# Per-row statistics and the tail copy as tensor_reduce, scores scaled at the PSUM copy, norm over 640 columns

## The chip, the cores and the metric

The kernel runs on one core of a Trainium2 chip. The metric is the device time in microseconds of one execution. The core has five engines that matter here: TensorE (PE, with its weight loads shown as PEld), VectorE (DVE), ScalarE (ACT), GpSimd (POOL) and the queue that issues DMAs (SP). Each runs its own instructions in order, and they meet at semaphores.

## The reference

Three stages follow each other. Attention has 4 batches of 8 heads, 576 rows and a head size of 64; it keeps only the 32 largest scores of each row:

```python
scores = scale * np.matmul(q, k.transpose(0, 1, 3, 2))      # scale = 1/8
kth = np.partition(scores, -top_k, axis=-1)[..., -top_k:-top_k + 1]
scores = np.where(scores >= kth, scores, -1000000000.0)
scores = scores - np.max(scores, axis=-1, keepdims=True)
attn = np.exp(scores)
attn = attn / (np.sum(attn, axis=-1, keepdims=True) + 1e-09)
out = np.matmul(attn, v)
```

Its output, 2304 tokens of 512 features, goes through a gated layer (`h = x @ w_in`, `h * sigmoid(h)`, `@ w_out`, inner width 2048), and then through `((x @ w1) * (x @ w2)) @ w3 @ w_out` with an inner width of 1024.

## The kernel before, in words

The 2304 tokens are cut into six blocks (`BLOCKS`) of three tiles of 128 rows. For each block the eight heads give 24 tiles of scores, taken two at a time: a **pair**, 72 of them in all. Blocks 0 and 1 are "native": their attention runs in plain float32. Blocks 2 to 5 split every operand into a rounded high part and a low rest, and multiply those.

The program writes its own order. `at(tick, order, fn)` puts a piece of work on a tick; a pair owns `SLOT = 7` ticks. After each tick the dense layers of the previous block (`mlp`, lines 645 to 647 for the first products of each layer, 766 for the last one) give a share of their steps, so that TensorE alternates between the two. During the first stretch these shares are the folding of `w3 @ w_out` (line 231) and the conversion of the weights (lines 134 to 202). After that, a scheduler in the compiler may still let an instruction pass another that would wait; each engine then runs the resulting list in order.

A pair goes through these steps:

- `plan_scores`: TensorE multiplies q and k (lines 412, 414, 415) into a PSUM bank, and `evac` (line 418) on ScalarE copies 288 columns into the score tile `st`.
- `plan_topk`, `mx` and `mr` (lines 445, 449) on VectorE: four rounds of MAX8 give the 32 largest values of a row in `top`, with three rounds of MATCH_REPLACE8 between them on the scratch tile `wk`.
- `bias` (lines 454, 455) on VectorE: `nt`, minus one eighth of the 32nd value, and `nb`, minus one eighth of the largest value less `nt`. Each handles 128 rows by 2 columns, a column for each tile of the pair.
- `mask` (line 463) and `ex` (line 469) on ScalarE: a Prelu with scale 1/8 and bias `nt` sends all that is below the 32nd value far down, and an Exp with bias `nb` follows, with the row's sum into `sm`.
- `recip` (lines 473, 474, 477) on VectorE: 1e-9 is added to `sm`, the reciprocal goes into `rc`; in the split blocks columns 512 to 575 of `e` times `rc` are written a second time, into columns 576 to 639.
- `norm` (lines 484, 486): columns 0 to 575 of `e` times `rc`, on ScalarE in the first four pairs and on GpSimd in the others.
- `plan_av`: two ticks or more later TensorE transposes `e` (lines 539 to 543), ScalarE copies it out (lines 549, 556, 557), GpSimd forms the low part (line 559), and TensorE multiplies with v (lines 572, 583).

GpSimd also forms the low parts of the dense layers' inputs (lines 660, 705), of q (line 335) and of k (line 340). All DMAs are issued by SP.

Of the kernel before, what the change touches and what calls it, by code (L numbers as in the profile page):

```python
# [8 lines left out]
FP32 = mybir.dt.float32  # L9
# [2 lines left out]
I32 = mybir.dt.int32  # L12
ACTF = mybir.ActivationFunctionType
ALU = mybir.AluOpType

TOPK = 32

# [12 lines left out]
SLOT = 7  # L30
NATIVE = lambda j: j < 2
# [19 lines left out]
def attention_moe_moe2_kernel(  # L51
# [13 lines left out]
    nc = tc.nc  # L65
    B, H, D2, S = qT.shape
# [7 lines left out]
    KC = (S + 127) // 128  # L74
    NFULL = S // 128
    HS = S // 2
    scale = 1.0 / float(D) ** 0.5
    NB = len(BLOCKS)

    w4_p = ctx.enter_context(tc.tile_pool(name="w4", bufs=1))  # L80
# [6 lines left out]
    s_p = ctx.enter_context(tc.tile_pool(name="s", bufs=2))  # L87
# [16 lines left out]
    def done(b):  # L104
        held.pop(id(b))
        free_banks.append(b)
# [4 lines left out]
    zero = w4_p.tile([128, 128], FP32R, name="zero")  # L111

    low = w4_p.tile([128, 1], FP32, name="low")
    n_conv = [0]


# [11 lines left out]
    def convert_scale(r, fold):  # L128
# [6 lines left out]
        else:  # L135
            nc.gpsimd.tensor_scalar(t, h, SHIFT, 1.0, op0=ALU.mult, op1=ALU.mult)

# [6 lines left out]
    def convert_bits(r, t_):  # L144
# [3 lines left out]
        nc.vector.scalar_tensor_tensor(out=wb, in0=tb, scalar=3, in1=r[:, :, 0],  # L148
                                       op0=ALU.logical_shift_left, op1=ALU.bitwise_or)
        if bits:  # L150
            nc.vector.scalar_tensor_tensor(out=wb, in0=r[:, :, 1], scalar=0x80000000, in1=wb,
                                           op0=ALU.bitwise_and, op1=ALU.bitwise_or)
        else:
            nc.gpsimd.tensor_tensor(out=w, in0=w, in1=r[:, :, 1].bitcast(FP32), op=ALU.mult)
        return w
# [122 lines left out]
    def at(tick, order, fn):  # L278
        plan.setdefault(tick, []).append((order, len(plan.get(tick, ())), fn))
# [110 lines left out]
    tiles = {}  # L390

    def plan_scores(n, base):
        items = []
        for j, h, i in pairs[n]:
            t0, T = blocks[j]
            for half in range(2):
                for si, (off, n_, b, s) in enumerate(runs(t0, T)):
                    a, e = max(off, i * 128), min(off + n_, (i + 1) * 128)
                    if a < e:
                        items.append((j, h, i, half, si, a - i * 128, e - i * 128))  # L400

        def go(tick, j, h, i, half, si, r0, r1):
            hd = heads[j, h]
            if n not in tiles:
                tiles[n] = s_p.tile([128, 2, S], FP32, tag="st", bufs=SB, name="st")
            m = pairs[n].index((j, h, i))
            kk = hd["k"][si][0]
            ps = bank("s")
            cs = slice(half * HS, (half + 1) * HS)
            q_ = hd["q"][:, i * 128:(i + 1) * 128]  # L410
            if NATIVE(j):
                nc.tensor.matmul(ps[:, 0:HS], lhsT=q_[0:D], rhs=kk[0:D, 0, cs], start=True, stop=True)  # L412
            else:
                nc.tensor.matmul(ps[:, 0:HS], lhsT=q_, rhs=kk[:, 0, cs], start=True, stop=False)  # L414
                nc.tensor.matmul(ps[:, 0:HS], lhsT=q_, rhs=kk[:, 1, cs], start=False, stop=True)  # L415

            def evac():
                nc.scalar.copy(out=tiles[n][r0:r1, m, cs], in_=ps[r0:r1, 0:HS])  # L418
                done(ps)

            at(tick + 1, 0, evac)

        for x, item in enumerate(items):
            tk = base + x * (SLOT - 1) // len(items)
            at(tk, 2, lambda tk=tk, item=item: go(tk, *item))

    def plan_topk(n, base):
        pr = pairs[n]
        m = len(pr)
        st = {}  # L430
        NR = TOPK // 8

        def begin():
            st["top"] = s_p.tile([128, 2, TOPK], FP32, tag="top", name="top")
            st["nt"] = s_p.tile([128, 2], FP32, tag="nt", name="nt")
            st["nb"] = s_p.tile([128, 2], FP32, tag="nb", name="nb")
            st["sm"] = s_p.tile([128, 2], FP32, tag="sm", name="sm")
            st["rc"] = s_p.tile([128, 2], FP32, tag="rc", name="rc")
            st["wk"] = s_p.tile([128, 2, S], FP32, tag="wk", bufs=1, name="wk")
            st["s"] = tiles[n]  # L440
            st["e"] = []

        def mx(r):
            for i in range(m):
                nc.vector.max(out=st["top"][:, i, r * 8:r * 8 + 8], in_=st["s" if r == 0 else "wk"][:, i])  # L445

        def mr(r):
            for i in range(m):
                nc.vector.match_replace(out=st["wk"][:, i], in_to_replace=st["top"][:, i, r * 8:r * 8 + 8],  # L449
                                        in_values=st["s" if r == 0 else "wk"][:, i], imm_value=-3.0e38)  # L450

        def bias():

            nc.vector.tensor_scalar(st["nt"][:, 0:m], st["top"][:, 0:m, TOPK - 1], -scale, 1.0, op0=ALU.mult, op1=ALU.mult)  # L454
            nc.vector.scalar_tensor_tensor(out=st["nb"][:, 0:m], in0=st["top"][:, 0:m, 0], scalar=-scale,  # L455
                                           in1=st["nt"][:, 0:m], op0=ALU.mult, op1=ALU.subtract)

        def mask():

            for i in range(m):  # L460
                e = s_p.tile([128, KC * 128], FP32, tag="e", bufs=EB, name="e")
                st["e"].append(e)
                nc.scalar.activation(out=e[:, 0:S], in_=st["s"][:, i], func=ACTF.Prelu, scale=scale,  # L463
                                     bias=st["nt"][:, i:i + 1], alpha=BELOW)

        def ex():
            for i in range(m):
                e = st["e"][i][:, 0:S]
                nc.scalar.activation(out=e, in_=e, func=ACTF.Exp, bias=st["nb"][:, i:i + 1],  # L469
                                     accum_out=st["sm"][:, i:i + 1])  # L470

        def recip():
            nc.vector.tensor_scalar(st["sm"][:, 0:m], st["sm"][:, 0:m], 1e-9, 1.0, op0=ALU.add, op1=ALU.mult)
            nc.vector.reciprocal(out=st["rc"][:, 0:m], in_=st["sm"][:, 0:m])  # L474
            for i in range(m):
                if not NATIVE(pr[i][0]):
                    nc.vector.tensor_scalar(st["e"][i][:, S:KC * 128], st["e"][i][:, NFULL * 128:S], st["rc"][:, i:i + 1], 1.0,
                                            op0=ALU.mult, op1=ALU.mult)

        def norm(i):  # L480
            e = st["e"][i]
            p = e[:, 0:S]
            if NORM_ACT(n):
                nc.scalar.activation(out=p, in_=p, func=ACTF.Copy, scale=st["rc"][:, i:i + 1])
            else:
                nc.gpsimd.tensor_scalar(p, p, st["rc"][:, i:i + 1], 1.0, op0=ALU.mult, op1=ALU.mult)  # L486
            j, h, t = pr[i]
            heads[j, h]["p"][t] = e
            tiles.pop(n, None)

        at(base, 1, begin)
        ops = []
        for r in range(NR):
            ops.append(lambda r=r: mx(r))
            if r < NR - 1:
                ops.append(lambda r=r: mr(r))
        for x, f in enumerate(ops):
            at(base + x * (SLOT - 1) // len(ops), 1.1, f)
        end = base + SLOT
        at(end - 1, 1.2, bias)  # L500
        at(end, 0, mask)
        at(end, 0.1, ex)
        at(end, 1.5, recip)
        for i in range(m):
            at(end + 1, 0.5, lambda i=i: norm(i))
# [317 lines left out]

    with ExitStack():
        make_identity(nc, ident)
        nc.gpsimd.memset(low, 7.5 * 2.0 ** -16 - 0.5)
        nc.gpsimd.memset(zero.bitcast(FP32), 0.0)
        start = min(plan)
        fs = fold_steps() + [lambda k=k: conv_step(k) for k in range(8)]
        side = Spread(fs, ready[0] - RO)  # L830
        j = -1
        tick = start
        while plan or j + 1 < NB:
            todo = plan.pop(tick, [])
            while todo:
                todo.sort(key=lambda x: x[:2])
                todo.pop(0)[2]()
                todo += plan.pop(tick, [])
            if tick >= FS:
                side.tick()  # L840
            if j + 1 < NB and tick == ready[j + 1]:
                side.rest()
                j += 1
                side = Spread(mlp(j), ready[j + 1] - ready[j] - MO if j + 1 < NB else 1)
            tick += 1
        side.rest()
# [44 lines left out]
```

## Time and profile before

| what | value |
|---|---|
| median of 3 runs | 1232.19 us (1224.46 to 1238.07) |
| the profiled execution | 1226.51 us, of which the span is 1224.7 us |
| mean granted TensorE clock in it | 0.975 |
| instructions | 19194 |
| busy: PE, DVE, ACT, POOL | 1143.9, 992.2, 852.3, 736.4 us |
| last score work on DVE | at about 1073 us; after it only the last block's dense layers are left |

The busy time of an engine is the union of its instructions' spans. On TensorE a matmul's span is longer than the distance to the next one, so small gaps do not show there. The chain of waits follows the work that ended last back to its start; its shares say on which engine time was spent that nothing else covered at that point, but they do not say how close a second path runs.

### The profile page before, as it was taken

To read this page: it belongs to the slowest core of one execution; us is meant where nothing else is said; L and a number is where in the kernel's file an instruction comes from. 1 tells how busy PE (TensorE), PEld (TensorE's weight loads), DVE (VectorE), ACT (ScalarE), POOL (GpSimd) and SP (SyncE) were. 2 spreads that over 40 slices of the span, in tenths; PEclk is the share of its full clock that TensorE was granted. 3 is DMA by queue.
4 is the path that set the end of the run, shared out by engine and by line. 5 is a ranking of instruction groups with operands and counts; after the bars stand their busy time and mean duration, and the time that the engine had idled before them with its cause. 6 is when DMAs were issued, how large, how long until landed. Compare 5 with 4: busy or idle time off the path is not lost.

```text
span 1224.7 us, 19194 instructions
## 1 busy us (share of the span) xinstructions
PE 1143.9 (93%) x6000; PEld 967.9 (79%) x6000; DVE 992.2 (81%) x2064; ACT 852.3 (70%) x1907; POOL 736.4 (60%) x744
## 2 busy tenths in 40 slices
PE   7798949799989999999999999999999999999998
PEld 4343424677767879999889999899899999999997
DVE  7997889989998988999989998978989999811100
ACT  5695677788897578887777878768867877642221
POOL 3453562787978357786577766667756666552221
PEclk9898978999999999999999999999999999999999
DMA  8642372678876466676678766887875775437741
GB/s 228 187 150 59 110 236 79 224 245 281 252 252 227 160 183 222 195 252 201 191 239 275 236 222 204 282 269 258 290 231 176 236 256 186 166 121 253 253 173 43
DMA packets 122502, 254.24 MB, mean 208 GB/s; under 512 B 40224, under 2 KB 63264, under 8 KB 122400
## 3 DMA queue, kind: packets, MB, share of 16 engines
q1 hardware_dynamic: 122400, 253.01, 63.3%
q8 instruction: 48, 0.79, 0.3%
q14 instruction: 54, 0.44, 0.1%
HBM read 206.31 MB, written 46.66 MB: 207 GB/s over the span
## 4 chain that ended last, share of the span: by engine, by line
PE 59%; DVE 22%; ACT 8%; DMA 3%; issue 3%; POOL 1%; ACTq 0%; DVEq 0%; POOLq 0%
PE bank L645 12%; PE bank L646 11%; PE bank L647 11%; DVE top L445 9%; PE bank L766 7%; DVE wk L449 7%; PE bank L231 3%; PE bank L572 3%; PE bank L539 3%; PE bank L583 3%; PE bank L412 3%; PE bank L414 1%; ACT e L463 1%; PE bank L415 1%; ACT e L469 1%
## 5 line engine op out<-in xcount | busy, mean ns | idle before, releaser
L445 DVE MAX8 top<-wk 128x8 f32<-128x576 f32 x432 | 319.4, 750 | 3.9
L660 POOL TENSOR_TENSOR gl<-gf,gh 128x384 fp32r<-128x384 f32 x144 | 148.9, 1037 | 135.4 <-ACT gh L659 130.8
L449 DVE MATCH_REPLACE8 wk<-top,wk 128x576 f32<-128x576 f32 x288 | 212.8, 740 | 0.0
L559 POOL TENSOR_TENSOR pl<-pf,ph 128x384 fp32r<-128x384 f32 x128 | 129.2, 1017 | 83.2 <-ACT ph L557 69.1
L418 ACT COPY st<-bank 128x288 f32<-128x288 f32 (+1 forms) x320 | 123.8, 403 | 62.4 <-PE bank L415 38.6
L486 POOL TENSOR_SCALAR e<-e,rc 128x576 f32<-128x576 f32 x136 | 105.3, 785 | 74.2 <-DVE rc L474 31.3
L445 DVE MAX8 top<-st 128x8 f32<-128x576 f32 x144 | 107.3, 748 | 38.4 <-ACT st L418 38.1
L645 PE MATMUL bank<-xh,wt 128*128 128x384 f32 x384 | 131.8, 346 | 6.9 <-DVE gf L687 3.5
L645 PE MATMUL bank<-x2h,wt 128*128 128x384 f32 x384 | 132.0, 348 | 1.9 <-ACT x2h L704 1.1
L646 PE MATMUL bank<-gl,wt 128*128 128x384 f32 x384 | 131.8, 343 | 0.3
L646 PE MATMUL bank<-x2l,wt 128*128 128x384 f32 x384 | 130.1, 339 | 1.1 <-POOL x2l L705 1.0
L646 PE MATMUL bank<-xl,wt 128*128 128x384 f32 x384 | 130.0, 338 | 0.0
L647 PE MATMUL bank<-xh,wt 128*128 128x384 f32 x384 | 129.9, 338 | 0.0
L647 PE MATMUL bank<-gh,wt 128*128 128x384 f32 x384 | 129.8, 338 | 0.0
L647 PE MATMUL bank<-x2h,wt 128*128 128x384 f32 x384 | 129.4, 337 | 0.0
L539 PE MATMUL bank<-ident,e 128*128 128x128 f32 x576 | 99.8, 281 | 30.3 <-POOL e L486 16.3
L463 ACT ACTIVATE e<-st,nt 128x576 f32<-128x576 f32 x144 | 104.3, 773 | 26.9 <-DVE nt L454 26.5
L539 PEld LDWEIGHTS bank<-ident,e 128*128 128x128 f32 x576 | 70.7, 142 | 56.0 <-POOL e L486 17.8
L469 ACT ACTIVATE e<-e,nb 128x576 f32<-128x576 f32 x144 | 111.4, 778 | 0.4 <-DVE nb L455 0.2
L659 ACT CAST gh<-gf 128x384 fp32r<-128x384 f32 x144 | 74.3, 519 | 52.4 <-DVE gf L754 38.2
L687 DVE SCALAR_TENSOR_TENSOR gf<-th,bank 128x384 f32<-128x384 f32 x96 | 51.8, 545 | 68.2 <-ACT th L682 67.1
L449 DVE MATCH_REPLACE8 wk<-top,st 128x576 f32<-128x576 f32 x144 | 106.2, 739 | 0.0
(93 smaller groups left out, 2951.3 us busy)
## 6 DMA issues: line engine op xcount, KB each, us to landing
wt<-scr SPq DMA_DIRECT2D x240, 512.0 KB, 4.3
scr<-wt SPq DMA_DIRECT2D x48, 512.0 KB, 4.0
raw<-in_w_dram SPq DMA_DIRECT2D x24, 512.0 KB, 4.3
k<-kk SPq DMA_DIRECT2D x16, 576.0 KB, 4.1
kk<-k SPq DMA_DIRECT2D x16, 576.0 KB, 5.1
raw<-in_w3T_dram SPq DMA_DIRECT2D x16, 512.0 KB, 4.7
raw<-in_w_in_dram SPq DMA_DIRECT2D x16, 512.0 KB, 4.4
raw<-in_w_out_dram SPq DMA_DIRECT2D x16, 512.0 KB, 4.3
```

The lines of the kernel that those rows point to most:

```text
L418: nc.scalar.copy(out=tiles[n][r0:r1, m, cs], in_=ps[r0:r1, 0:HS])
L445: nc.vector.max(out=st["top"][:, i, r * 8:r * 8 + 8], in_=st["s" if r == 0 else "wk"][:, i])
L449: nc.vector.match_replace(out=st["wk"][:, i], in_to_replace=st["top"][:, i, r * 8:r * 8 + 8], in_values=st["s" if r == 0 else "wk"][:, i], ...
L463: nc.scalar.activation(out=e[:, 0:S], in_=st["s"][:, i], func=ACTF.Prelu, scale=scale, bias=st["nt"][:, i:i + 1], alpha=BELOW)
L469: nc.scalar.activation(out=e, in_=e, func=ACTF.Exp, bias=st["nb"][:, i:i + 1], accum_out=st["sm"][:, i:i + 1])
L486: nc.gpsimd.tensor_scalar(p, p, st["rc"][:, i:i + 1], 1.0, op0=ALU.mult, op1=ALU.mult)
L539: nc.tensor.transpose(ps[:, i * 128:(i + 1) * 128], p[:, kc * 128:kc * 128 + 128], ident)
L559: nc.gpsimd.tensor_sub(out=pl[f], in0=pf[f], in1=ph[f])
L645: nc.tensor.matmul(ps, lhsT=wh, rhs=rh, start=first, stop=False)
L646: nc.tensor.matmul(ps, lhsT=wh, rhs=rl, start=False, stop=False)
L647: nc.tensor.matmul(ps, lhsT=wl, rhs=rh, start=False, stop=last)
L660: nc.gpsimd.tensor_sub(out=u["l"], in0=full, in1=u["h"])
```

## The change

Every small VectorE operation of `bias` and `recip` but the reciprocal becomes a `tensor_reduce` with one input. `nt` is the negated 32nd value; a new operation `negmax` writes the negated maximum into a 33rd column of `top`, early in the pair; `nb` is the sum of columns 32 and 33. The 1e-9 stands in the second column of a tile `sums` that is set once at the start and used in rotation by four pairs; a reduction over two columns adds it to the row's sum. The tail copy of 64 columns is a reduction over an axis of length one, stands ahead of the reciprocal, and copies values that are not yet multiplied; GpSimd's norm covers 640 columns instead of 576 in the split blocks. The factor 1/8 moves from these operations and from the Prelu into the copy out of PSUM, which becomes an activation with a scale.

```diff
+AX = mybir.AxisListType.X
+    sums = w4_p.tile([128, 4, 2, 2], FP32, name="sums")
...
-                nc.scalar.copy(out=tiles[n][r0:r1, m, cs], in_=ps[r0:r1, 0:HS])
+                nc.scalar.activation(out=tiles[n][r0:r1, m, cs], in_=ps[r0:r1, 0:HS], func=ACTF.Copy, scale=scale)
...
-            st["top"] = s_p.tile([128, 2, TOPK], FP32, tag="top", name="top")
+            st["top"] = s_p.tile([128, 2, TOPK + 1], FP32, tag="top", name="top")
-            st["sm"] = s_p.tile([128, 2], FP32, tag="sm", name="sm")
+            st["sm"] = sums[:, n % 4]
...
+        def negmax():
+            nc.vector.tensor_reduce(out=st["top"][:, 0:m, TOPK], in_=st["top"][:, 0:m, 0:1], axis=AX, op=ALU.add, negate=True)
+
         def bias():
-            nc.vector.tensor_scalar(st["nt"][:, 0:m], st["top"][:, 0:m, TOPK - 1], -scale, 1.0, op0=ALU.mult, op1=ALU.mult)
-            nc.vector.scalar_tensor_tensor(out=st["nb"][:, 0:m], in0=st["top"][:, 0:m, 0], scalar=-scale,
-                                           in1=st["nt"][:, 0:m], op0=ALU.mult, op1=ALU.subtract)
+            nc.vector.tensor_reduce(out=st["nt"][:, 0:m], in_=st["top"][:, 0:m, TOPK - 1:TOPK], axis=AX, op=ALU.add, negate=True)
+            nc.vector.tensor_reduce(out=st["nb"][:, 0:m], in_=st["top"][:, 0:m, TOPK - 1:TOPK + 1], axis=AX, op=ALU.add)
...
-                nc.scalar.activation(out=e[:, 0:S], in_=st["s"][:, i], func=ACTF.Prelu, scale=scale,
+                nc.scalar.activation(out=e[:, 0:S], in_=st["s"][:, i], func=ACTF.Prelu,
                                      bias=st["nt"][:, i:i + 1], alpha=BELOW)
...
-                                     accum_out=st["sm"][:, i:i + 1])
+                                     accum_out=st["sm"][:, i, 0:1])
...
         def recip():
-            nc.vector.tensor_scalar(st["sm"][:, 0:m], st["sm"][:, 0:m], 1e-9, 1.0, op0=ALU.add, op1=ALU.mult)
-            nc.vector.reciprocal(out=st["rc"][:, 0:m], in_=st["sm"][:, 0:m])
             for i in range(m):
                 if not NATIVE(pr[i][0]):
-                    nc.vector.tensor_scalar(st["e"][i][:, S:KC * 128], st["e"][i][:, NFULL * 128:S], st["rc"][:, i:i + 1], 1.0,
-                                            op0=ALU.mult, op1=ALU.mult)
+                    nc.vector.tensor_reduce(out=st["e"][i][:, S:KC * 128], in_=st["e"][i][:, NFULL * 128:S].unsqueeze(2),
+                                            axis=AX, op=ALU.add)
+
+            nc.vector.tensor_reduce(out=st["rc"][:, 0:m], in_=st["sm"][:, 0:m], axis=AX, op=ALU.add)
+            nc.vector.reciprocal(out=st["rc"][:, 0:m], in_=st["rc"][:, 0:m])
...
-            p = e[:, 0:S]
+            p = e[:, 0:S] if NATIVE(pr[i][0]) else e
...
+        at(base + 2 * (SLOT - 1) // len(ops), 1.15, negmax)
...
+        nc.gpsimd.memset(sums, 1e-9)
```

## Rows read from the trace of the kernel before

**Rows 1.** The page's head and part 1: busy time, share and instructions of each engine.

```profile
span 1224.7 us, 19194 instructions
PE 1143.9 (93%) x6000; PEld 967.9 (79%) x6000; DVE 992.2 (81%) x2064; ACT 852.3 (70%) x1907; POOL 736.4 (60%) x744
```

**Rows 2.** The page, part 4: the chain of waits, shares by engine and by line.

```profile
PE 59%; DVE 22%; ACT 8%; DMA 3%; issue 3%; POOL 1%; ACTq 0%; DVEq 0%; POOLq 0%
PE bank L645 12%; PE bank L646 11%; PE bank L647 11%; DVE top L445 9%; PE bank L766 7%; DVE wk L449 7%; PE bank L231 3%; PE bank L572 3%; PE bank L539 3%; PE bank L583 3%; PE bank L412 3%; PE bank L414 1%; ACT e L463 1%; PE bank L415 1%; ACT e L469 1%
```

**Rows 3.** Busy time by stretch: first 400 us, and from there to the end of attention.

```profile
core 0: us, PE busy (x) PEld busy (x) DVE busy (x) ACT busy (x) POOL busy (x), PEclk, DMA share, GB/s
0.00:400.00 400.00, 345.41 (x1319) 212.34 (x1320) 358.35 (x687) 298.83 (x617) 246.61 (x233) 0.93 0.61 195
400.00:1075.00 675.00, 654.99 (x3892) 618.59 (x3891) 619.05 (x1351) 512.15 (x1204) 446.77 (x469) 1.00 0.68 224
```

**Rows 4.** DVE groups by line: count, busy us, mean ns, idle before, releaser.

```profile
L449 DVE MATCH_REPLACE8 wk<-top,wk 128x576 f32<-128x576 f32 x288 | 212.8, 740 | 0.0
...
L477 DVE TENSOR_SCALAR e<-e,rc 128x64 f32<-128x64 f32 x96 | 36.1, 416 | 0.4
L454 DVE TENSOR_SCALAR nt<-top 128x2 f32<-128x2 f32 x72 | 32.6, 453 | 1.4
L455 DVE SCALAR_TENSOR_TENSOR nb<-top,nt 128x2 f32<-128x2 f32 x72 | 29.6, 412 | 0.4
...
L473 DVE TENSOR_SCALAR sm<-sm 128x2 f32<-128x2 f32 x72 | 23.9, 331 | 14.1 <-ACT e L469 13.9
...
L474 DVE RECIPROCAL rc<-sm 128x2 f32<-128x2 f32 x72 | 10.8, 150 | 0.4
```

**Rows 5.** Single lines of DVE: shortest, median and longest duration in ns.

```profile
L454 DVE TENSOR_SCALAR nt<-top x72: 143/331/1346, 22.1 to 1067.7; 128x2 f32<-128x2 f32 x72
L474 DVE RECIPROCAL rc<-sm x72: 136/150/167, 30.0 to 1071.8; 128x2 f32<-128x2 f32 x72
L477 DVE TENSOR_SCALAR e<-e,rc x96: 228/248/1099, 420.7 to 1073.2; 128x64 f32<-128x64 f32 x96
```

**Rows 6.** Timeline of DVE near 701 us: start, duration.

```profile
701.32 1.19 DVE L477 TENSOR_SCALAR e<-e,rc 128x64 f32<-128x64 f32 x2
...
703.94 0.76 DVE L445 MAX8 top<-wk 128x8 f32<-128x576 f32 x1
704.74 0.67 DVE L454 TENSOR_SCALAR nt<-top 128x2 f32<-128x2 f32 x1
```

**Rows 7.** Timeline of POOL in the same stretch.

```profile
701.29 1.01 POOL L335 TENSOR_TENSOR qs<-qr,qs 64x384 fp32r<-64x384 f32 x1
...
703.96 1.43 POOL L340 TENSOR_TENSOR kk<-kr,kk 128x576 fp32r<-128x576 f32 x1
```

**Rows 8.** Single lines of ACT: shortest, median and longest duration in ns.

```profile
L418 ACT COPY st<-bank x320: 368/398/514, 5.7 to 1061.2; 128x288 f32<-128x288 f32 x129, 64x288 f32<-64x288 f32 x31
L418 ACT ACT_TABLE_LOAD  x1: 1283/1283/1283, 0.7 to 0.7; - x1
...
L748 ACT COPY a<-bank x48: 452/480/524, 361.3 to 1212.7; 128x384 f32<-128x384 f32 x48
...
L682 ACT ACTIVATE th<-bank x96: 467/492/538, 213.9 to 1163.5; 128x384 f32<-128x384 f32 x96
L703 ACT ACTIVATE gf<-bank x24: 469/532/637, 344.3 to 1170.0; 128x384 f32<-128x384 f32 x24
```

**Rows 9.** POOL by line: the norm.

```profile
L486 POOL TENSOR_SCALAR e<-e,rc 128x576 f32<-128x576 f32 x136 | 105.3, 785 | 74.2 <-DVE rc L474 31.3 <-DVE e L477 19.3 <-ACT gh L659 10.9
```

**Rows 10.** Who waited for whom: total us, times, longest us.

```profile
DVE top L445 <- ACT st L418: 38.1, 24, 7.1
...
PEld bank L539 <- POOL e L486: 17.8, 5, 16.0
PE bank L539 <- POOL e L486: 16.3, 2, 15.7
```

## The prediction

> **What bounds the kernel now.** I read the head of the page first [rows 1]. No engine is idle enough to be ignored, and none is full: TensorE is busy 1143.9 us of 1224.7 and VectorE 992.2. VectorE's work stops with the attention, near 1075 us, so the share of 81% misleads. By stretch [rows 3] VectorE is busy 358.35 of the first 400 us and 619.05 of the 675 us after them, 90% and 92%; TensorE is busy 345.41 and 654.99, 86% and 97%. TensorE therefore idles 54.6 us early and 20.0 us later, and those 74.6 us are about all that anything off TensorE can give back. Early the granted clock is 0.93, later 1.00: the idle time lies where some clock is missing too.
>
> The chain of waits says who made TensorE wait [rows 2]. It runs 59% on TensorE, 22% on VectorE, 8% on ScalarE and 1% on GpSimd. 22% of 1224.7 us is 269 us, or 0.27 us of chain for each of VectorE's 992.2 busy us. MAX8 and MATCH_REPLACE8 are 9% and 7% of the chain, but the 6% left on VectorE are other lines. I use 0.27 as the weight of a saved VectorE microsecond, and call it an assumption: a second path may run close behind.
>
> Then the groups that the change replaces [rows 4]: four lines cost 36.1 + 32.6 + 29.6 + 23.9 = 122.2 us, an eighth of VectorE, and three of them handle two columns. Their means of 453, 412 and 331 ns stand beside 150 ns for the reciprocal, which is just as small. Shortest, median and longest tell why [rows 5]: `nt` takes from 143 to 1346 ns, the reciprocal never more than 167. So it is not the size; something holds the one form and not the other. The timelines show what [rows 6, 7]. Two tail copies start at 701.32 and take 1.19 us together, while a GpSimd subtraction runs from 701.29 to 702.30. `nt` starts at 704.74 and takes 0.67 us, ending at 705.41; GpSimd's subtraction ends at 705.39. The MAX8 at 703.94 takes its usual 0.76 us although GpSimd works from 703.96 on. A TENSOR_SCALAR waits for GpSimd's instruction to finish; a MAX8 does not, nor does a reciprocal.
>
> **The change part by part.**
>
> Small VectorE operations. There were 3 x 72 of two columns; now there are 4 x 72, with `negmax`. No row shows a tensor_reduce. The nearest is the reciprocal: one input in SBUF, two columns, 150 ns [rows 4]. I take it, so 288 x 0.150 = 43.2 us. The lower end is its shortest, 136 ns [rows 5], 39.2 us. The upper end is that a tensor_reduce is held as its predecessors were: the 86.1 us of the three lines over 216 instructions are 399 ns, times 288 is 114.8 us.
>
> Tail copies, 96 of 64 columns. Between the reciprocal's two columns at 150 ns and MATCH_REPLACE8's 576 at 740 [rows 4] a column costs 1.03 ns, so 64 cost 150 + 62 x 1.03 = 214 ns and all 20.5 us; upper end the present mean of 416 ns, 39.9 us; lower end 200 ns from the shortest reciprocal, 19.2 us. The free form takes 228 ns at best now [rows 5], so I expect no faster copy, only one that isn't held.
>
> Here a rule speaks against the change. The Trainium skill ("VectorE: DVE Perf Modes", The perf-mode tier table) gives tensor_reduce only the plain rate, and a float32 tensor_scalar in SBUF twice that. By the page the copy would be slower by 32 cycles, an estimate of 33 ns; on the median of 248 ns that makes 281 ns, 27.0 us for all and 1.8 us more on the path than my sum.
>
> The sum on VectorE: 122.2 - 43.2 - 20.5 = 58.5 us saved, 63.8 at the lower prices, and 32.5 us lost at the upper ones. On the path, at 0.27: 15.9 us gained, between 17.2 gained and 8.8 lost.
>
> Whether a tensor_reduce is held at all no row shows; the Trainium skill ("SBUF — State Buffer", Who interferes with whom) says that on this chip it never contends with GpSimd for their shared ports, which would exclude the upper end. That is not used in the sum.
>
> Order of the small ones. `nb` no longer needs `nt`, and the copies no longer need `rc`, so two dependent steps go; I count nothing for them, as other pairs' MAX8 usually stand between. `negmax` follows the first MAX8 on its own engine and waits for nobody. The copies stand ahead of the reciprocal and keep both norms of a pair for 2 x 214 ns; the norm waited for them already, behind `sm` and `rc`, so this is free while they are short.
>
> Scores out of PSUM, 320 copies on ScalarE, COPY to an activation with scale. At 384 columns a COPY has a median of 480 ns, a Tanh with scale 492, and a Copy with scale 532 [rows 8]: 12 to 52 ns more. I take 52, the same function: 320 x 0.052 = 16.6 us busy. ScalarE has 8% of the chain, 98 us for 852.3 busy, a weight of 0.115: 1.9 us lost; at 12 ns 0.4. The function is in use already with one table load in the whole run [rows 8], so no load comes with it. The Prelu without a scale keeps its work: nothing.
>
> Norm over 640 columns, 96 on GpSimd. 785 ns for 576 [rows 9], so 64 more cost at most 785 x 64/576 = 87 ns, 8.4 us. GpSimd has 1% of the chain, 12 us for 736.4 busy: 0.1 us. The lower end is nothing.
>
> `sums`: one memset at the start, beside the first loads; the row sum of a pair overwrites what was read four pairs earlier: nothing. No DMA is added or moved, and SP's queue stays as it is.
>
> In all 15.9 - 1.9 - 0.1 = 13.9 us faster. The profiled execution took 1226.51 us and would take 1212.6. The median of the runs is 1232.19, 5.7 us above it, so the forecast for the runs is **1218 us**.
>
> **The rivals.**
>
> *TensorE covers it.* From 400 us on TensorE is 97% busy [rows 3], and most of the 58.5 us falls there: the 36.1 - 20.5 = 15.6 us of the copies, the first of which starts at 420.7 [rows 5], and of the 42.9 left the share of the split blocks' 48 pairs out of 72, 44 us in all. VectorE would reach the next pair's scores earlier and wait there; it already waits 38.1 us in 24 places for the score copies, which now get longer [rows 10]. Against it: 54.6 us of idle time early. Half the weight, 7.9 less 2, gives 6 us: 1226. Chance 0.22.
>
> *VectorE bounds more than the chain shows.* It is busy at least 90% in both stretches, and a held instruction also delays all behind it. At twice the weight 31.6 less 2 gives 30 us: 1202. For it: 74.6 us of TensorE's time to be had. Against it: only 20.0 of them after 400 us. Chance 0.18.
>
> *The norm comes later and the transposes wait (slower).* If copies and sum stay as long as now, the first norm of a pair follows 2 x 416 + 399 + 150 = 1381 ns after the row sums, where 331 + 150 + 416 = 897 ns stand now; with two longer norms that is 484 + 174 = 658 ns, for 48 pairs 31.6 us. It decides from the point where a transpose starts less than that behind its norm; with half the pairs there it costs 16 us: 1248. Against it: TensorE waits for the norm 16.3 us in 2 places and 17.8 for weight loads in 5, nearly all in one gap of about 16 us [rows 10], so there is slack nearly everywhere. Chance 0.07.
>
> *It does not do what it says.* A tensor_reduce is held by GpSimd like the others: 8.8 + 2 us lost, 1243. Against it, the reciprocal's and MAX8's behaviour. Chance 0.05.
>
> **How the numbers follow.** My forecast has 0.48, with its own range of 1208 to 1226. A difference under 1%, 12.3 us, can't be told from none here, as three runs alone spread by 13.6; faster means below 1219.9, slower above 1244.5. The forecast lies near that bound, and I put 0.32 of its 0.48 below it; with 0.18 from the larger gain and 0.02 from the first rival, faster has 0.52. Slower has the late norm's 0.07 and 0.02 of the last rival, 0.09. The same has 0.39. The range reaches over the larger gain to 1196 and over the first rival to 1238, which leaves out the two slow cases and the tail of the large gain.
>
> **What would show it.** Right: `nt`, `nb`, `negmax` and the sum at about 150 ns in the mean and none near 1 us; copies near 214 ns; VectorE's busy time near 934 us; score copies by 52 ns longer; the norm below 875 ns; TensorE's idle time before 1075 us smaller by 14 us, and the chain's VectorE share lower. Wrong: small operations still several hundred ns in the mean (held all the same), or VectorE's time gone with its waits for the score copies up by as much (covered), or transposes waiting for the norm in many places. A lower granted clock in the first stretch, or another order of the instructions by the compiler's scheduler, would be outside all of this.

## The result

The changed kernel takes 1212.18 us (median of 4 runs, 1208.94 to 1213.67) where the kernel before took 1233.49 beside it: a ratio of 0.9855, 95% interval 0.9806 to 0.9904. A second comparison, with 23 runs of the kernel before, gave 1209.77 against 1225.99, ratio 0.9862 [0.9837, 0.9887]; by that ratio the change saves 16.9 us, between 13.9 and 20.0. The plain quotients of the medians, 0.983 and 0.987, lie inside the two intervals; the ratios are used below. The forecast was 13.9 us less, which is the lower end. The profiled execution took 1213.67 us, 12.8 less than the profiled one of before.

The head of the page after, part 1 and part 4 (the chain of waits), to be held against [rows 1, 2]:

```profile
span 1211.8 us, 19237 instructions
PE 1141.2 (94%) x6000; PEld 972.9 (80%) x6000; DVE 931.3 (77%) x2136; ACT 853.0 (70%) x1907; POOL 745.7 (62%) x745
...
PE 72%; DVE 9%; ACT 8%; DMA 5%; POOL 4%; issue 2%; SPq 0%; ACTq 0%; POOLq 0%; DVEq 0%
```

VectorE has 72 more instructions and is busy 60.9 us less; its share of the chain fell from 22% to 9%, and TensorE's rose from 59% to 72%. Now VectorE's groups of the kernel after, columns as in [rows 4]:

```profile
L479 DVE TENSOR_REDUCE e<-e 128x64 f32<-128x64 f32 x96 | 20.0, 209 | 19.4 <-ACT e L473 19.1
L483 DVE RECIPROCAL rc<-rc 128x2 f32<-128x2 f32 x72 | 11.0, 152 | 0.4
L459 DVE TENSOR_REDUCE nt<-top 128x2 f32<-128x2 f32 x72 | 10.8, 150 | 1.2
L460 DVE TENSOR_REDUCE nb<-top 128x2 f32<-128x4 f32 x72 | 10.6, 148 | 0.0
L482 DVE TENSOR_REDUCE rc<-sums 128x2 f32<-128x4 f32 x72 | 10.5, 146 | 8.0 <-ACT e L473 6.9 <-ACT st L420 1.1
L455 DVE TENSOR_REDUCE top<-top 128x2 f32<-128x2 f32 x72 | 10.5, 145 | 0.0
```

The 122.2 us of the old forms became 62.4. The single lines, shortest, median and longest in ns, as in [rows 5]:

```profile
L459 DVE TENSOR_REDUCE nt<-top x72: 128/154/157, 23.1 to 1053.2; 128x2 f32<-128x2 f32 x72
...
L479 DVE TENSOR_REDUCE e<-e x96: 198/208/222, 416.0 to 1056.3; 128x64 f32<-128x64 f32 x96
```

No `nt` is longer than 157 ns where one took 1346, and no copy longer than 222 where one took 1099. The two things that the change pays with, score copies and norm, by line:

```profile
L491 POOL TENSOR_SCALAR e<-e,rc 128x640 f32<-128x640 f32 x96 | 75.9, 804 | 12.6 <-DVE rc L483 11.9
...
L420 ACT ACTIVATE st<-bank 128x288 f32<-128x288 f32 (+1 forms) x320 | 128.4, 414 | 62.3 <-PE bank L417 36.9
```

To see where the time went I cut the span where the attention of block 1 and that of block 5 end: at the start of the block's last conversion of `xh`, the input of its dense layers, on ScalarE. Columns as in [rows 3]; first the kernel before, then the one after:

```profile
0.00:438.70 438.70, 384.11 (x1526) 243.22 (x1527) 391.00 (x763) 322.21 (x670) 260.64 (x248) 0.93 0.60 190
438.70:1099.70 661.00, 640.99 (x3826) 610.86 (x3825) 588.07 (x1278) 499.52 (x1175) 445.39 (x467) 1.00 0.68 225
```

```profile
0.00:434.20 434.20, 381.96 (x1526) 246.16 (x1527) 374.74 (x789) 322.48 (x671) 264.25 (x249) 0.93 0.60 192
434.20:1085.70 651.50, 639.99 (x3826) 613.08 (x3825) 543.38 (x1324) 499.95 (x1175) 450.24 (x466) 0.99 0.68 228
```

TensorE does the same work in each stretch (1526 and 3826 matmuls), so the lengths can be compared: blocks 0 and 1 are 4.5 us shorter, blocks 2 to 5 are 9.5 us shorter. What follows block 5's attention takes 125 to 126 us in both.

### The profile page after: what moved, and what is told of

The parts are those of the page before. It is cut to its first block, busy times and chain, and to the rows that moved or that the text cites. A ratio compares the mean times of both kernels' runs of the same rounds, so it can differ in the third digit from the quotient of the medians.

```text
span 1211.8 us, 19237 instructions
## 1 busy us (share of the span) xinstructions
PE 1141.2 (94%) x6000; PEld 972.9 (80%) x6000; DVE 931.3 (77%) x2136; ACT 853.0 (70%) x1907; POOL 745.7 (62%) x745
## 4 chain that ended last, share of the span: by engine, by line
PE 72%; DVE 9%; ACT 8%; DMA 5%; POOL 4%; issue 2%; SPq 0%; ACTq 0%; POOLq 0%; DVEq 0%
PE bank L651 14%; PE bank L652 14%; PE bank L653 14%; PE bank L772 8%; PE bank L589 4%; PE bank L578 4%; PE bank L545 4%; DVE top L447 3%; PE bank L233 3%; DVE wk L451 3%; PE bank L414 3%; PE bank L416 2%; PE bank L417 2%; DVE w L150 1%; DMA raw<-in_w_dram 1%
## 5 line engine op out<-in xcount | busy, mean ns | idle before, releaser
L666 POOL TENSOR_TENSOR gl<-gf,gh 128x384 fp32r<-128x384 f32 x144 | 151.8, 1055 | 149.0 <-ACT gh L665 145.6
L420 ACT ACTIVATE st<-bank 128x288 f32<-128x288 f32 (+1 forms) x320 | 128.4, 414 | 62.3 <-PE bank L417 36.9
L491 POOL TENSOR_SCALAR e<-e,rc 128x640 f32<-128x640 f32 (+1 forms) x136 | 110.4, 824 | 54.7 <-DVE rc L483 47.6
L447 DVE MAX8 top<-st 128x8 f32<-128x576 f32 x144 | 108.0, 752 | 40.4 <-ACT st L420 39.9
L545 PE MATMUL bank<-ident,e 128*128 128x128 f32 x576 | 98.5, 282 | 18.0 <-POOL e L491 12.8
```

The lines of the kernel that those rows point to most:

```text
L420: nc.scalar.activation(out=tiles[n][r0:r1, m, cs], in_=ps[r0:r1, 0:HS], func=ACTF.Copy, scale=scale)
L545: nc.tensor.transpose(ps[:, i * 128:(i + 1) * 128], p[:, kc * 128:kc * 128 + 128], ident)
L666: nc.gpsimd.tensor_sub(out=u["l"], in0=full, in1=u["h"])
```

## The experiments

All kernels below are variants of the changed one unless they say otherwise; ratios are to the kernel before.

**Tail copy alone in the old form.**

```diff
-                    nc.vector.tensor_reduce(out=st["e"][i][:, S:KC * 128], in_=st["e"][i][:, NFULL * 128:S].unsqueeze(2),
-                                            axis=AX, op=ALU.add)
+                    nc.vector.tensor_scalar(st["e"][i][:, S:KC * 128], st["e"][i][:, NFULL * 128:S], 1.0, 1.0,
+                                            op0=ALU.mult, op1=ALU.mult)
```

> The changed kernel with only the tail copies of 64 columns back in the old form (a TENSOR_SCALAR by 1.0, still ahead of the reciprocal). Theory (GpSimd holds this form, and VectorE's time counts on the path): mean of the copy from 209 back to about 400 ns, 96 x 0.2 = 19 us more on VectorE, 5 to 7 us more in the time: about 1218 us. Rival 1 (TensorE covers VectorE's time, the gain came from elsewhere): copy as long, time within 3 us of 1212. Rival 2 (the norm waits for the copies): the time goes up by more than 10 us and the transposes wait for the norm in more places.

Measured: 1216.96 us, ratio 0.9919 [0.9892, 0.9947]; over the changed kernel's 0.9862 that is 1.0058, 7 us. The line in its profile:

```profile
L479 DVE TENSOR_SCALAR e<-e 128x64 f32<-128x64 f32 x96 | 30.6, 318 | 16.8 <-ACT e L473 16.0
```

109 ns more for each copy, 10.6 us in all, half of what was expected (the old mean of 416 ns is not back), yet the time came out as expected. With intervals of 3 us on either side the one sum can't judge the weight; it does say that the copy's form has a part in the gain.

**Two-column operations alone in the old forms.**

```diff
-  nc.vector.tensor_reduce(out=st["nt"][:, 0:m], in_=st["top"][:, 0:m, TOPK - 1:TOPK], axis=AX, op=ALU.add, negate=True)
-  nc.vector.tensor_reduce(out=st["nb"][:, 0:m], in_=st["top"][:, 0:m, TOPK - 1:TOPK + 1], axis=AX, op=ALU.add)
+  nc.vector.tensor_scalar(st["nt"][:, 0:m], st["top"][:, 0:m, TOPK - 1], -1.0, 1.0, op0=ALU.mult, op1=ALU.mult)
+  nc.vector.scalar_tensor_tensor(out=st["nb"][:, 0:m], in0=st["top"][:, 0:m, 0], scalar=-1.0,
+                                 in1=st["nt"][:, 0:m], op0=ALU.mult, op1=ALU.subtract)
...
-  nc.vector.tensor_reduce(out=st["rc"][:, 0:m], in_=st["sm"][:, 0:m], axis=AX, op=ALU.add)
+  nc.vector.tensor_scalar(st["rc"][:, 0:m], st["sm"][:, 0:m, 0], 1e-9, 1.0, op0=ALU.add, op1=ALU.mult)
...
-  at(base + 2 * (SLOT - 1) // len(ops), 1.15, negmax)
```

> The changed kernel with only the operations on two columns back in the old forms (TENSOR_SCALAR, SCALAR_TENSOR_TENSOR, TENSOR_SCALAR; no negmax). Theory: means back to 330 to 450 ns, 86 - 42 = 44 us more on VectorE, at 0.27 to 0.35 us of time for each 12 to 15 us more: about 1225 us. Rival 1 (covered): within 3 us of 1212. With copy_held the two losses should add up to the 21 us between the kernels; if both are near zero the order of the instructions made the gain.

Measured: 1220.79 us, ratio 0.9941 [0.9911, 0.997]; over 0.9862 that is 1.0080, 9.7 us, a little under what was expected. Its groups:

```profile
L460 DVE SCALAR_TENSOR_TENSOR nb<-top,nt 128x2 f32<-128x2 f32 x72 | 31.6, 439 | 0.4
L459 DVE TENSOR_SCALAR nt<-top 128x2 f32<-128x2 f32 x72 | 30.9, 429 | 1.2
...
L483 DVE TENSOR_SCALAR rc<-sums 128x2 f32<-128x2 f32 x72 | 22.2, 308 | 1.4 <-ACT e L474 1.4
```

The old means, 453, 412 and 331 ns [rows 4], are nearly back, with nothing else of the old kernel. The two losses, 7.0 and 9.7 us, add up to 16.7 of the 16.9 us between the kernels, each with an interval of some 3 us to either side. Each edit also gave the instructions another order, copy_held from about 418 us on and small_held from 28 us on, and what that did is inside the two losses.

**The two prices of the change taken away** (left out: the factor 1/8 on the scores, and the norm of the copied tail).

```diff
-  nc.scalar.activation(out=tiles[n][r0:r1, m, cs], in_=ps[r0:r1, 0:HS], func=ACTF.Copy, scale=scale)
+  nc.scalar.copy(out=tiles[n][r0:r1, m, cs], in_=ps[r0:r1, 0:HS])
...
-  p = e[:, 0:S] if NATIVE(pr[i][0]) else e
+  p = e[:, 0:S]
```

> The changed kernel without the two terms priced as losses: the scores come out of PSUM by COPY without the factor 1/8, and the norm covers 576 columns (left out: the scaling of the scores, the norm of the copied tail). Theory by the durations after (414 against 403 ns for the score copies, 804 ns for 640 columns): ScalarE 4 us and GpSimd 5 us less busy, 0 to 1 us of time: about 1211 us. By the prediction's prices 2 us. Rival (the compiler's order moves the time more than such terms): a change of 4 us or more either way.

Measured: 1212.04 us, ratio 0.987 [0.9846, 0.9893] beside 0.9862 for the changed kernel: nothing to be seen, so the two prices are worth under some 3 us. The order of the instructions changed here too, from about 530 us on, and no change of the time came of it either.

**VectorE's saved time spent again.** Three reductions that nobody uses, for each pair, one in `bias` and two in `recip`; first for all pairs, then for those of blocks 0 and 1 (`pr[0][0] < 2`), then for the others (`>= 2`).

```diff
+    spent = w4_p.tile([128, 1], FP32, name="spent")
...
+        def spend():
+            nc.vector.tensor_reduce(out=spent, in_=ident, axis=AX, op=ALU.add)
```

> The changed kernel with VectorE's saved time spent again in a form that isn't held: three useless reductions over 128 columns for each pair, one ahead of nt and two ahead of the tail copies, 216 x 0.28 = 60 us. Theory (it is VectorE's time as such that counts): 16 to 21 us slower than the changed kernel, about 1231 us, the same as the kernel before. Rival (it is the holding, through GpSimd's own work or the irregular delays, not the sum of the time): under 6 us slower, at most 1218.

> As time_back, with the useless reductions only in the 24 pairs of blocks 0 and 1: 72 x 0.27 = 20 us more on VectorE, all in about the first 400 us. From the profile of time_back, where the attention of block 1 ended 23 us later than in the changed kernel and the later blocks took no longer. Theory (VectorE's time counts in full there): about 20 us slower than the changed kernel. Rival (an even weight of 0.27 to 0.35 over the whole run): 5 to 7 us slower.

> As time_back, with the useless reductions only in the 48 pairs of blocks 2 to 5: 144 x 0.27 = 39 us more on VectorE after about 400 us. Theory (TensorE covers it there): within 3 us of the changed kernel. Rival (an even weight): 10 to 14 us slower.

Measured: 1237.41 us, ratio 1.0075 [1.0044, 1.0105]; 1224.99 us, 0.9988 [0.9958, 1.0018]; 1231.68 us, 1.0032 [1.0004, 1.006]. Against 0.9862 that is 26, 15 and 21 us slower. The third is the opposite of what I expected, and the reason stands in its profile: the reductions by stretch, with VectorE's busy time and their count in brackets.

```profile
0.00:451.50 451.50, 39.27 (x144) 0.92 0.58 185
451.50:1102.90 651.40, 0.00 (x0) 1.00 0.68 227
```

All 144 ran before block 1 was done, the first 1.5 us after the start. They read a constant tile and wait for nothing, so the scheduler put them in front. My reading of the first of the three, that later blocks don't feel VectorE's time, was therefore wrong when I wrote the expectations of the other two: none of the three put any time there. What they do show is that work on VectorE in the first 450 us is dear: block 1's attention ended at 447.0, 451.5 and 457.0 us instead of 429.7 and 434.2 (two profiles of the changed kernel), for 20, 39 and 59 us of such reductions. That is 0.4 to 0.9 us for each us of reductions. It includes the other order of the instructions and a lower granted clock: these first stretches hold 65, 72 and 85 us in which TensorE ran at the lower of its two clock levels, 1.2 GHz instead of 2.4, where the changed kernel's hold 58 in either profile. The runs do not separate the three.

**The changed kernel again**, for the interval.

> The changed kernel itself, beside the kernel before on one chip, for a narrower interval. Expected: 0.986 of the kernel before, as in the first comparison; its two rivals are gains of 0.98 and of 0.992, both inside that first interval.

Measured: ratio 0.9862 [0.9837, 0.9887], as expected; neither rival is inside.

**Fewer operations still.**

```diff
-            nc.vector.tensor_reduce(out=st["nb"][:, 0:m], in_=st["top"][:, 0:m, TOPK - 1:TOPK + 1], axis=AX, op=ALU.add)
...
-                nc.scalar.activation(out=e, in_=e, func=ACTF.Exp, bias=st["nb"][:, i:i + 1],
-                                     accum_out=st["sm"][:, i, 0:1])
+                nc.scalar.activation(out=e, in_=e, func=ACTF.Exp, accum_out=st["sm"][:, i:i + 1])
...
-            nc.vector.tensor_reduce(out=st["rc"][:, 0:m], in_=st["sm"][:, 0:m], axis=AX, op=ALU.add)
-            nc.vector.reciprocal(out=st["rc"][:, 0:m], in_=st["rc"][:, 0:m])
+            nc.vector.reciprocal(out=st["rc"][:, 0:m], in_=st["sm"][:, 0:m])
...
-        at(base + 2 * (SLOT - 1) // len(ops), 1.15, negmax)
```

> The changed kernel with three of its five small operations left out: rows are shifted by their 32nd largest score instead of the largest (softmax does not change with the shift; nb and negmax go), and 1e-9 is not added to the row sums, which are at least 32 so that float32 does not hold it (the sum over two columns goes). 216 x 0.147 = 32 us less on VectorE, 10.6 of them in blocks 0 and 1. Theory (time counts in full in the first two blocks and not later): 8 to 11 us faster than the changed kernel. Rival 1 (even weight of 0.27 to 0.35): 9 to 11 us, which the time does not tell apart, but then the later blocks are shorter by 6 us or more. Rival 2 (TensorE covers all by now): under 3 us.

Measured: 1209.48 us, ratio 0.9866 [0.9839, 0.9893], the same as the changed kernel. Its two stretches:

```profile
0.00:420.60 420.60, 377.74 (x1521) 240.29 (x1522) 368.46 (x709) 317.20 (x670) 265.49 (x249) 0.95 0.62 198
420.60:1080.00 659.40, 644.55 (x3836) 620.09 (x3835) 537.04 (x1187) 494.07 (x1176) 449.51 (x465) 0.99 0.68 225
```

Blocks 0 and 1 are 9 us and more shorter than the changed kernel's, blocks 2 to 5 about 8 us longer, although VectorE is busy less in both. Two things in the profiles bear on this. First, VectorE's busy time fell by 11 to 13 us, to 918.6 from 931.3 and 929.7 in the two profiles of the changed kernel, and not by the 32 of the expectation. Neighbouring instructions' spans overlap (in the changed kernel the durations add up to 1037.7 us where the engine is busy 931.3), so leaving out an instruction of 147 ns saves less than 147 ns of the engine. At 0.27 that asks for some 3 us of time, which the interval can't tell from none, so the sum doesn't choose among the expectations. Second, the granted clock lies otherwise. In blocks 2 to 5 TensorE ran 17 us at its lower level, 1.2 GHz, where the changed kernel's two profiles have 7 and 3; in blocks 0 and 1 it was 41 us against 58. If a stretch at half the clock loses at most half of its length, my estimate from these figures is that the clock can account for 5 to 7 us of the longer later blocks and for 8 of the shorter early ones. What lowered it there, and the rest, stay open. No version here beats the changed kernel clear of the noise.

**Another order of the instructions, for both kernels.** The same reductions in the last 8 pairs of the changed kernel (`if n >= 64`), in the last 8 and the last 12 of the kernel before. They too turned out to run at the start (24 in the first 30 us, 36 in the first 59), so they are a small load there, and a new order for all the rest.

> The changed kernel with three useless reductions over 128 columns in the last 8 pairs alone (24 x 0.27 = 6.5 us on VectorE near the end, where spend_split showed VectorE's time to be covered). Their only other effect is that the compiler's scheduler puts the instructions of the whole program in another order from the 21st matmul on, as it did for the three kernels with useless reductions. Theory (that other order lengthened blocks 0 and 1, not VectorE's time): the attention of block 1 ends more than 10 us later than the changed kernel's 430 to 434 us, blocks 2 to 5 take 648 to 653 us as in all kernels without held operations, and the time is 10 to 20 us above the changed kernel's. Rival (the useless reductions did it): block 1 ends at 430 to 436 us and the time is within 4 us.

> The kernel before with the same 24 useless reductions in its last 8 pairs, which gives it, too, another order from the 26th matmul on. Theory: blocks 0 and 1 move by up to 20 us either way with the order; blocks 2 to 5 take 655 to 662 us, as with the held operations in the kernel before, small_held and copy_held, 4 to 10 us more than order_new. Rival (the order made those differences also): blocks 2 to 5 anywhere between 648 and 662 us.

> As order_old_64, with the useless reductions in the last 12 pairs (36 x 0.27 = 9.8 us): a third order of the kernel before. The same expectations: blocks 2 to 5 at 655 to 662 us by the theory; the end of block 1 anywhere within 20 us.

Measured: 1215.98 us, ratio 0.99 [0.9867, 0.9934]; 1235.91 us, 1.0064 [1.0042, 1.0087]; 1245.78 us, 1.0148 [1.0099, 1.0197]. Blocks 2 to 5 of the three, one line from each kernel:

```profile
437.50:1090.10 652.60, 638.92 (x3825) 610.89 (x3825) 544.19 (x1323) 502.04 (x1175) 448.70 (x465) 1.00 0.68 227
```

```profile
441.10:1105.40 664.30, 644.16 (x3828) 613.71 (x3827) 593.49 (x1282) 501.33 (x1175) 444.58 (x467) 0.99 0.67 223
```

```profile
451.90:1117.40 665.50, 644.28 (x3830) 613.20 (x3829) 591.89 (x1282) 500.98 (x1176) 445.15 (x467) 1.00 0.67 223
```

The first two carry the same load and differ by 0.9900/1.0064 = 0.984: the gain is there in another pair of orders as well. In the later blocks 652.6 stands against 664.3 and 665.5 us, as the theory said, and a little beyond its range. The end of block 1, 437.5, 441.1 and 451.9 us, moves with the order: the two variants of the old kernel differ there by 10.8 us, for 3.2 us of reductions, with 61 and 72 us at the lower clock up to there. For order_new the expectation was mostly wrong: block 1 ended 3 to 8 us later than in the changed kernel, not more than 10, and the time is 4.7 us above it by the ratios, between the theory and its rival. That expectation rested on the misread runs above.

**The forms by themselves** (no part of the computation).

```python
for _ in range(24):                        # and so on, form by form
    nc.vector.tensor_scalar(b, a[:, :, 0], -1.0, 1.0, op0=ALU.mult, op1=ALU.mult)
...
for _ in range(140):
    nc.gpsimd.tensor_sub(out=z, in0=x, in1=y)      # 128x576, beside the second pass
```

> No part of the computation: 24 of each form on VectorE with GpSimd idle, then the same with GpSimd subtracting 128x576 tiles without a pause; then 24 score copies of 288 columns out of PSUM as COPY and as activation with a scale. Theory: with GpSimd idle all two-column forms at 136 to 170 ns and the 64-column copy near 230 (TENSOR_SCALAR) and 210 ns (TENSOR_REDUCE); with GpSimd busy the TENSOR_SCALAR and SCALAR_TENSOR_TENSOR wait up to 1.4 us each, TENSOR_REDUCE and RECIPROCAL not at all. ScalarE: the activation 10 ns longer than COPY by the changed kernel's rows, 52 by the prediction. Rival: TENSOR_REDUCE over an axis of one is held too, or the two-input form is not.

Its groups by line; lines 90, 92 and 98 ran with GpSimd idle (but for the first instruction of 90 and of 98), lines 104 to 114 beside GpSimd's subtractions (line 120):

```profile
L120 POOL TENSOR_TENSOR z<-x,y 128x576 f32<-128x576 f32 x140 | 195.5, 1396 | 11.0
L112 DVE TENSOR_SCALAR tl<-e 128x64 f32<-128x64 f32 x24 | 31.2, 1299 | 0.0
L104 DVE TENSOR_SCALAR b<-a 128x2 f32<-128x2 f32 x24 | 17.1, 711 | 0.8
L106 DVE SCALAR_TENSOR_TENSOR b<-a 128x2 f32<-128x2 f32 x24 | 16.9, 703 | 0.8
L126 ACT ACTIVATE st<-ps 128x288 f32<-128x288 f32 x24 | 9.9, 411 | 0.8
L124 ACT COPY st<-ps 128x288 f32<-128x288 f32 x24 | 9.6, 399 | 0.8
...
L114 DVE TENSOR_REDUCE tl<-e 128x64 f32<-128x64 f32 x24 | 5.3, 220 | 0.0
L98 DVE TENSOR_SCALAR tl<-e 128x64 f32<-128x64 f32 x24 | 5.0, 208 | 1.0 <-POOL a L84 1.0
L90 DVE TENSOR_SCALAR b<-a 128x2 f32<-128x2 f32 x24 | 4.1, 171 | 0.0
...
L108 DVE TENSOR_REDUCE b<-a 128x2 f32<-128x4 f32 x24 | 3.8, 157 | 0.8
...
L92 DVE SCALAR_TENSOR_TENSOR b<-a 128x2 f32<-128x2 f32 x24 | 3.6, 150 | 0.0
L94 DVE TENSOR_REDUCE b<-a 128x2 f32<-128x4 f32 x24 | 3.5, 144 | 0.0
```

The passes did not stay apart: line 94, the two-column tensor_reduce of the idle pass, ran while GpSimd was at work, but for its first instruction. Single lines, shortest, median and longest in ns, then the first and the last start in us; GpSimd works from 14.8 us on:

```profile
L98 DVE TENSOR_SCALAR tl<-e x24: 195/195/514, 2.4 to 8.0; 128x64 f32<-128x64 f32 x24
L100 DVE TENSOR_REDUCE tl<-e x24: 220/220/220, 8.2 to 14.1; 128x64 f32<-128x64 f32 x24
L94 DVE TENSOR_REDUCE b<-a x24: 143/144/148, 14.5 to 45.0; 128x2 f32<-128x4 f32 x24
L104 DVE TENSOR_SCALAR b<-a x24: 169/707/1332, 52.6 to 70.3; 128x2 f32<-128x2 f32 x24
L112 DVE TENSOR_SCALAR tl<-e x24: 194/1439/1445, 14.6 to 45.1; 128x64 f32<-128x64 f32 x24
```

Beside GpSimd a TENSOR_SCALAR of two columns goes from 171 to 711 ns in the mean, the two-input form from 150 to 703, the copy from 208 to 1299. The two-column means mix two kinds: of the 24 of either form 12 took over 1.2 us, and each of these ended 16 to 26 ns after the end of one of GpSimd's subtractions; the other 12 took 160 to 171 ns. The copy as a tensor_reduce takes 220 ns with GpSimd idle (line 100) and 220 beside it (line 114). For two columns this run has no idle pass of the tensor_reduce: 144 and 157 ns were both taken beside GpSimd. The trace of the changed kernel has both cases: of its 288 two-column reductions 161 lie wholly inside a GpSimd instruction, with a mean of 147 ns, and 89 touch none, with a mean of 148. So the theory holds, and no rival. The activation costs 12 ns more than COPY.

## Why the prediction was right, and where it was not

**The hold by GpSimd.** Right, and shown three times. The forms alone show it. So does putting them back: the two-column operations come near their old means, the copy to 318 ns of its old 416. (That variant's copy multiplies by a constant where the old one multiplied by `rc`, and its copies under 300 ns take 192 ns in the mean against the old kernel's 244.) The trace of the kernel before shows it too: of the 312 operations of the four lines 136 took over 250 ns (tail copies: over 300), and every one of these ended 15 to 56 ns after the end of a GpSimd instruction. The new prices were 150 and 214 ns; measured were 145 to 150 and 209. VectorE's busy time was forecast near 934 us and is 931.3. The Trainium skill ("SBUF — State Buffer", Who interferes with whom) says that tensor_reduce never contends with GpSimd on this chip; 147 against 148 ns in the changed kernel and 220 against 220 alone agree. The upper ends, on which the last rival stood, are excluded.

**The rule that speaks against the change.** Alone, the copy's median is 195 ns as TENSOR_SCALAR and 220 as TENSOR_REDUCE. The Trainium skill's plain rate for tensor_reduce ("VectorE: DVE Perf Modes", The perf-mode tier table) made that 33 ns by my estimate; it is 25, in the direction of the rule. In the kernel there was no such loss: the old copy, which multiplies by `rc`, takes 228 ns at best [rows 5] and 416 in the mean with the hold, the reduction 209.

**The weight of 0.27.** The sum came out, at the edge: 13.9 us forecast, 16.9 measured with an interval of 13.9 to 20.0. For blocks 2 to 5 the weight itself can be read from the profiles, VectorE's busy time there against their length, both in us:

| kernels | VectorE busy | length |
|---|---|---|
| before, order_old_64, order_old_60 | 588.1, 593.5, 591.9 | 661.0, 664.3, 665.5 |
| small_held | 565.0 | 655.2 |
| copy_held | 551.4 | 656.0 |
| after, after_again, cost_terms, order_new | 543.4, 543.4, 545.5, 544.2 | 651.5, 650.4, 652.4, 652.6 |
| time_back, spend_native, spend_split (reductions all earlier) | 543.7, 543.6, 543.3 | 648.7, 649.3, 651.4 |
| no_max | 537.0 | 659.4 |

The three kernels with all the old forms have a mean of 591.2 and 663.6, the seven without them 543.9 and 650.9: 12.7 us for 47.3, or 0.27. That is across several orders of the instructions. Part by part it is less clear: copy_held lies 3 us above the line (5.1 us longer for 7.5 us of VectorE's time), small_held 1.4 below. The last row, no_max, lies some 10 us above it, of which its lower clock can account for 5 to 7 and the rest is open. Whether time that VectorE loses for another reason would cost as much there is open: the runs that were to tell placed none there. In blocks 0 and 1 VectorE saves 16 to 18 us, and they end 4.5 to 9 us earlier, at 58 us of lower clock in all three profiles; the order alone can move that end by several us, so there the share of the change is not settled. So the weight is shown for the whole and for the later blocks. That the sum fits although the two prices of the change did not show and single parts lie off the line is in part luck.

**Score copies.** The step that was mis-sized: 52 ns more each, 1.9 us on the path, from the copy with a scale in line 703 [rows 8]. The rise is 11 ns in the kernel and 12 alone; the lower end, from the Tanh, was the right row. Together with the norm it can't be seen in the time.

**The norm.** 804 ns for 640 columns, under the 875 that was forecast; the same 96 norms took 748 ns before, so 56 more each where 87 were allowed for. The transposes wait for it 12.8 us in 2 places, as before nearly all in one gap [rows 10], so the late norm did not happen:

```profile
DVE top L447 <- ACT st L420: 39.9, 29, 7.3
...
PE bank L545 <- POOL e L491: 12.8, 2, 12.5
```

**TensorE covers it.** VectorE's wait for score copies went from 38.1 to 39.9 us: it was not given back there. But most of the 60.9 us saved on VectorE did turn into waits, in places that the rival did not name. First two lines of the kernel before, then the same of the one after (columns as in [rows 10]):

```profile
DVE gf L687 <- ACT th L682: 67.1, 24, 7.8
DVE gf L754 <- PE bank L647: 61.2, 13, 8.8
```

```profile
DVE gf L693 <- ACT th L688: 79.3, 40, 7.5
DVE gf L760 <- PE bank L653: 74.1, 21, 9.5
```

These are the gate and the product in the dense layers, 25 us more; waits for the Exp grew by 12 (13.9 to 26.0), and those of the product for its copied factor `a` by 5 (11.9 to 17.3). TensorE's idle time up to the end of attention fell by 10.8 us in this profile and by 13.8 in that of after_again, where I named 14. In the changed kernel 63.8 us are left, 52.2 of them in the first 400 us:

```profile
0.00:400.00 400.00, 347.76 (x1340) 218.18 (x1341) 345.08 (x712) 300.45 (x620) 251.01 (x235) 0.93 0.61 194
400.00:1060.00 660.00, 648.49 (x3869) 617.32 (x3868) 571.37 (x1398) 510.54 (x1198) 451.17 (x468) 0.99 0.69 229
```

The larger gain of 30 us did not come: after 400 us TensorE is busy 98% and has 11.5 us left to give.

## What to carry to other kernels

Where a small operation has a mean far above its shortest time, look at what the neighbouring engine does during its long ones, and compare with another form of the same size: here the form and not the size or the count cost 60 us of one engine. As a first estimate, price a saved microsecond by the engine's share of the chain over its busy time; it held here for the change as a whole (16.9 of 60.9 us, or 0.28), not for each part of it. Compare the granted clock of two stretches before you give their difference to an engine. And when you add load to test a price, hang it on data of the stage that you mean and look where it ran before you read the time: what waits for nothing is moved to the start, and brings another order of everything else.

## What was not expected of the hardware

GpSimd pays next to nothing for the hold: in forms_alone the first 50 subtractions of 128x576, most of them beside VectorE's held forms, took a mean of 1399 ns, and the 79 after VectorE was done 1395; from one start to the next it is 1473 ns alone and, but for the first, at most 1484 beside them. The two-input form is held as much as the one-input form (703 and 711 ns).
